# Weight pieces' transfers asked for one piece earlier, and narrowing steps placed anew, in a retention and two-layer MoE kernel

## The chip, the cores and the metric

One core of a Trainium2 chip runs the whole program. The metric is the device time of one execution in microseconds; below that of a kernel stands the median of several runs. Lower is better.

## What is computed

Retention over 4 batches and 8 heads (576 positions, 64 per head), then two dense layers with a hidden width of 2048 on 2304 tokens of width 512. The weights arrive as 64-bit floats, because a float32 array times a float64 scalar gives one.

```python
def _attn_ref(q, k, v):                       # q, k, v: (4, 8, 576, 64)
    scores = scale * np.matmul(q, k.transpose(0, 1, 3, 2))
    gamma = 1.0 - 2.0 ** (-5.0 - np.arange(H))
    Dmat = np.where(rel >= 0, gamma[:, None, None] ** rel[None, :, :], 0.0)
    return np.matmul(scores * Dmat[None], v)

x = attn_out.transpose(0, 2, 1, 3).reshape(2304, 512)
h = x @ w_in;  x = np.maximum(0.01 * h, h) @ w_out      # first layer
h = x @ w2_in; x = (h - np.tanh(h)) @ w2_out            # second layer
```

## The kernel before

The kernel has two stages. `retention()` goes through 16 pairs of heads (`order`, pair 0 to 15). `layers()` then does the two dense layers. The change touches the first stage alone.

**A pair.** For pair i TensorE computes the scores (`scores`, L674), the chunk states (`states_mm`, L723, and `scores_tail`), and the outputs of pair i - 1 (L755, L766). DVE masks the scores (`mask`, L697), carries the states (L733) and, with ACT (L774), writes the output as a high and a low part (`finish`, L775). POOL scales q (`prep_q`, L642), ACT scales k of the next pair (`prep_k`, L658). One PSUM tile holds the scores of one pair, so scores i wait for mask i - 1.

**Units.** From pair 6 on (`first = NP + 2`) every pair also carries one unit of the first dense layer on finished tokens: `unit_h(u)` (L822, 24 matmuls into the PSUM tile x_b), its two evacuations on ACT (L828, L829) and one on DVE (L830), then `unit_o(u - 1)` (L847, 24 matmuls) and `unit_evac(u - 1)` (L864, or L866 on ACT and L867 on DVE). There is one x_b, so unit u + 1 needs L830 of unit u. Units 2 and 3 are the first to use the w1i and w1o pieces 2 and 3: their first 12 matmuls take piece 2, their last 12 piece 3.

**Weight pieces.** A piece is a 128 x 512 block of 64-bit weights, 512 KB. Piece keys are (layer, kind, f), kind 0 for w_in, 1 for w_out. Each goes through these steps: `load_piece` (a transfer on SP's queue, L147), `begin` (ACT, L164), `clamp` (DVE, L170), `shift` (DVE, L175), `top` and `low` (DVE, both L181), then the split: a high part on ACT (L253) and a low part on POOL (L254). Eight pieces of the first layer come first (`pieces`), then eight of the second layer (`early_kept`), which are split and written back to DRAM (`keep_split`, `keep_out`). Raw pieces are staged in parts of `acc` that are free yet: four places for the first eight, of which two serve the kept ones too, so a transfer has to wait for `low` of the piece that had the place before.

**Order.** Every engine and SP's DMA queue work strictly in the order in which the program writes the instructions. All steps of all pieces stand in one list, `ops`, made by `piece_ops(keys, ahead)`, which puts the transfer of the piece `ahead` further on right behind each piece's `low`. `fill(i, part)` issues the next stretch of the list at three points of pair i: part 0 after the mask and before the pair's other work (ahead of `unit_h`), part 1 between `unit_h` and `unit_o`, part 2 at the end. How far it goes is given by `marks` or, where it has an entry, by the table `early`: (i, part) -> index in the list.

On SP the transfers of pair i + 2 (q, k at L627 and L628; kv at L634 and L635) are written at the start of pair i. There are three kv buffers, so those of pair i + 2 wait for the outputs of pair i - 1, late in pair i; all that SP has behind them waits too.

Of the kernel before, what the change touches and what calls it, by code (L numbers as in the profile page):

```python
# [35 lines left out]
def retention_moe_moe(  # L36
# [101 lines left out]
    def load_piece(key):  # L138
        m, kind, f = key
        src = ((w1i, w1o), (w2i, w2o))[m][kind][f]  # L140
        if key in early_kept or key[0] == 0 and key[2] < GF:
            k = len(raw_at)
            raw_at[key] = at = NT - (2048 if k in (0, 1, 4, 5) else 1024)
            st = acc_t[:, k % 2 * 2 + 1, at:at + (1024 if wide else 512)].bitcast(I64 if wide else F32)
        else:
            st = pools["st"].tile([P, 512], I64 if wide else F32, tag="st", name="st")
        nc.sync.dma_start(out=st, in_=src)  # L147
        raw[key] = st

    def narrow_ops(key):  # L150

        if not wide:
            def only():
                w = cw_pool[0].tile([P, 512], F32, tag="cw", name="cw")
                nc.vector.tensor_copy(out=w, in_=raw.pop(key))
                half[key] = w
            return [only]
        t = {}

        def begin():  # L160
            words = raw.pop(key).bitcast(U32).rearrange("p (n t) -> p n t", t=2)
            t["lo"], t["hi"] = words[:, :, 0], words[:, :, 1]
            t["w"] = cw_pool[0].tile([P, 512], U32, tag="cw", name="cw")
            nc.scalar.activation(  # L164
                out=t["w"].bitcast(F32), in_=t["hi"].bitcast(F32), func=AF.Abs
            )

        def clamp():
            wf = t["w"].bitcast(F32)
            nc.vector.tensor_scalar(  # L170
                out=wf, in0=wf, scalar1=F64_LO, scalar2=F64_HI, op0=ALU.max, op1=ALU.min
            )

        def shift():
            nc.vector.tensor_scalar(  # L175
                out=t["w"], in0=t["w"], scalar1=3, scalar2=0x3FFFFFF8,
                op0=ALU.logical_shift_left, op1=ALU.bitwise_and,
            )

        def join(src, scalar, op):  # L180
            nc.vector.scalar_tensor_tensor(  # L181
                out=t["w"], in0=t[src], scalar=scalar, in1=t["w"], op0=op, op1=ALU.bitwise_or
            )

        def top():
            join("hi", 0xC0000000, ALU.bitwise_and)

        def low():
            join("lo", 29, ALU.logical_shift_right)
            half[key] = t["w"].bitcast(F32)  # L190

        return [begin, clamp, shift, top, low]
# [11 lines left out]
    def keep_ops(key):  # L204

        m, kind, f = key
        if kind:
            return [([lambda: keep_split(key, half.pop(key))], [lambda: keep_out(key)])]
        stages = [([lambda: keep_split(key, half[key])], [lambda: keep_out(key)])]
        if f % 2:  # L210
            both = [(0, f - 1), (1, f - 1)]
            stages[0][1].append(lambda: sums_of(f - 1))
            stages.append((
                [lambda k=k: keep_split(k, half.pop((1, 0, f - 1 + k[0]))) for k in both],
                [lambda k=k: keep_out(k) for k in both],
            ))
        return stages
# [24 lines left out]
    def split_piece(key):  # L242
        wf = half.pop(key)
        m, kind, f = key
        if kind:
            wp = w_out_place(m)
        else:
            wp = w_place(m, f // GF, f % GF)
        split_into(wp, wf)
        wt[key] = wp  # L250
# [7 lines left out]
    early_kept = [(1, 1, f) for f in range(GF, 3 * GF)]  # L258
# [276 lines left out]
    def piece_ops(keys, ahead=2, split=True, spare=()):  # L535


        ops, later = [], []

        def due():  # L540
            soon = [x for stages in later for x in stages[:1]]
            later[:] = [stages[1:] for stages in later if stages[1:]]
            return [op for x, _ in soon for op in x], [op for _, x in soon for op in x]

        for j, key in enumerate(keys):
            part = narrow_ops(key)
            if j + ahead < len(keys):
                part.append(lambda k=keys[j + ahead]: load_piece(k))
            soon, then = due()
            ops += part[:3] + soon + part[3:] + then  # L550
            if key in spare:
                later.append(keep_ops(key))
            elif split:
                later.append([([lambda k=key: split_piece(k)], [])])
        while later:
            soon, then = due()
            ops += soon + then
        return ops


    def retention():
        with ExitStack() as ac:
# [22 lines left out]
            def factors(p, n):  # L585
                at, parts = 0 if p == 0 else LONE, []
                for width in (16, 32, 8, 16):
                    parts.append(tab_sb[:, at:at + width * n])
                    at += width * n
                return parts  # L590

            kt_sb = []
            for p, n in ((0, 1), (1, NP - 1)):
                k = factors(p, n)[0].rearrange("p (n h a) -> p n h a", h=2, a=8)
# [6 lines left out]
            order = [(b, p) for b in range(B) for p in range(NP)]  # L601
# [18 lines left out]
            def load(i):  # L620
                load_qk(i)
                load_v(i)
# [15 lines left out]
            def prep_q(i):  # L638

                b, p = order[i]  # L640
                q = qk[i][:, 1, :MAIN].rearrange("p (c r) -> p c r", r=CH)
                nc.gpsimd.tensor_tensor(  # L642
                    out=q, in0=q, in1=qt_sb[:, p:p + 1, :].to_broadcast([P, NFULL, CH]),
                    op=ALU.mult,
                )
                if i < GROUPED:
                    prep_q_tail(i)
# [19 lines left out]
            def scores(i):  # L667
                kt, qt = qk[i][:, 0, :], qk[i][:, 1, :]
                sc = ps_s.tile([P, 2, 512], F32, tag="sc", name="sc")
                for c in range(NFULL):  # L670
                    cs = slice(c * CH, (c + 1) * CH)
                    for h in range(2):
                        r = slice(64 * h, 64 * h + 64)
                        nc.tensor.matmul(  # L674
                            out=sc[:, h, cs], lhsT=kt[r, cs], rhs=qt[r, cs], start=True, stop=True
                        )
                return sc
# [93 lines left out]
            def finish(i, src, lo, hi):  # L771
# [6 lines left out]


            pieces = [(0, kind, f + j) for f in range(0, GF, 2) for kind in range(2) for j in range(2)]  # L780
            base = len(piece_ops(pieces, ahead=3))
            ops = piece_ops(pieces, ahead=3) + [lambda k=k: load_piece(k) for k in early_kept[:2]]
            ops += piece_ops(early_kept, spare=early_kept)
            at_pair = [0, 4, 9, 15, 22, 34, 46, 52]
            marks = [0] + at_pair + [
                base + 2 + (len(ops) - base - 2) * i // (len(order) - 8) for i in range(len(order) - 7)
            ]
            first = NP + 2
            done, u = [0], 0

            early = {
# [3 lines left out]
            }  # L795

            def fill(i, part):
                a, b = marks[i:i + 2] if i < len(order) else marks[-1:] * 2
                now = early.get((i, part), a + (b - a) * (part + 1) // 3)
                for op in ops[done[0]:now]:  # L800
                    op()
                done[0] = max(done[0], now)
# [66 lines left out]
            def pair_steps(i, fast):  # L869
# [46 lines left out]
                base=0, channel_multiplier=-1,  # L916
# [23 lines left out]
            def busy(n):  # L940
                for _ in range(n):
                    nc.tensor.matmul(
                        out=x_b[:, 0, :CH], lhsT=tri, rhs=tri, start=True, stop=True
                    )

            busy(8)
            for i in range(len(order)):
                if i + 2 < len(order):
                    load(i + 2)
                if i < 2:  # L950
                    load_piece(pieces[i + 1])
                fast = i >= first
                sc = scores(i)
                if i == 0:
                    busy(4)
                prep_q(i)
                mask(i, sc)
                if i == 0:
                    mask_table(1, NP - 1)
                fill(i, 0)  # L960
                pair_steps(i, fast)
                if fast or (i, 2) in early:
                    fill(i, 2)
# [250 lines left out]
```

## Time and profile before

| | before |
|---|---|
| median of 3 runs | 868.64 us (867.55 to 869.42) |
| profiled execution | 867.3 us, of it the span 865.4 us |
| mean granted TensorE clock over the span | 0.994 |
| TensorE matmul busy | 848.4 us, 98% of the span |
| DVE, ACT, POOL busy | 70%, 51%, 44% |

Times in the rows are microseconds from the start of the span. The granted clock is given as a share of 2.4 GHz: 1.00 is that level, 0.50 is 1.2 GHz. "Pair i" below is the stretch from the first score matmul of pair i to that of pair i + 1: pair 8 runs from 47.56 to 59.61, pair 9 to 69.92, pair 10 to 88.90, pair 11 to 98.40.

### The profile page before, as it was taken

To read this page: it belongs to the slowest core of one execution; us is meant where nothing else is said; L and a number is where in the kernel's file an instruction comes from. 1 tells how busy PE (TensorE), PEld (TensorE's weight loads), DVE (VectorE), ACT (ScalarE), POOL (GpSimd) and SP (SyncE) were. 2 spreads that over 40 slices of the span, in tenths; PEclk is the share of its full clock that TensorE was granted. 3 is DMA by queue.
4 is the path that set the end of the run, shared out by engine and by line. 5 is a ranking of instruction groups with operands and counts; after the bars stand their busy time and mean duration, and the time that the engine had idled before them with its cause. 6 is when DMAs were issued, how large, how long until landed. Compare 5 with 4: busy or idle time off the path is not lost.

```text
span 865.4 us, 15316 instructions
## 1 busy us (share of the span) xinstructions
PE 848.4 (98%) x5774; PEld 752.8 (87%) x5774; DVE 608.9 (70%) x1052; ACT 445.6 (51%) x879; POOL 377.3 (44%) x308
## 2 busy tenths in 40 slices
PE   8996999999999999999999999999999999999997
PEld 7886999988888889888888989888999899999996
DVE  7994876597877676659675487856766667777775
ACT  4542443453345433453544477766656556665664
POOL 4432232050035401464355477755555455454454
PEclk9997999999999999999999999999999999999999
DMA  9853754242355534553544603392225412563112
GB/s 354 305 175 113 224 180 159 100 133 97 122 189 208 186 123 123 219 195 122 195 171 154 210 1 148 140 346 79 88 89 184 172 74 74 195 243 123 49 50 73
DMA packets 37784, 133.77 MB, mean 155 GB/s; under 512 B 4304, under 2 KB 4944, under 8 KB 35664
## 3 DMA queue, kind: packets, MB, share of 16 engines
q1 hardware_dynamic: 37424, 132.66, 43.1%
q8 instruction: 45, 0.74, 0.4%
q14 instruction: 27, 0.22, 0.1%
q10 hardware_dynamic: 288, 0.15, 0.1%
HBM read 96.62 MB, written 36.18 MB: 153 GB/s over the span
## 4 chain that ended last, share of the span: by engine, by line
PE 91%; DVE 4%; issue 2%; DMA 1%; POOL 1%; ACT 1%; SPq 0%; DVEq 0%; POOLq 0%; ACTq 0%
PE a L426 41%; PE h L273 22%; PE h L307 18%; PE x_b L822 3%; PE a L847 3%; PE o L766 1%; PE o L755 1%; PE sc L674 1%; DVE cw L181 1%; DMA qk<-in_kT 1%; DVE pt L697 1%; DMA acc<-in_w2o 1%; PE x_c L723 0%; DVE st L733 0%; POOL w L254 0%
## 5 line engine op out<-in xcount | busy, mean ns | idle before, releaser
L426 PE MATMUL a<-w 128*128 128x512 f32 (+1 forms) x1680 | 394.1, 377 | 0.0
L426 PEld LDWEIGHTS a<-w 128*128 128x128 f32 x1680 | 293.4, 188 | 47.4
L254 POOL TENSOR_TENSOR w<-cw,w 128x512 fp32r<-128x512 f32 x80 | 113.6, 1438 | 253.6 <-ACT w L253 227.9
L273 PE MATMUL h<-xh,w 128*128 128x512 f32 (+1 forms) x672 | 187.1, 349 | 0.0
L366 POOL TENSOR_TENSOR v<-t,u 128x512 f32<-128x512 f32 (+1 forms) x76 | 93.3, 1228 | 98.3 <-ACT t L363 94.2
L273 PEld LDWEIGHTS h<-xh,w 128*128 128x128 f32 x672 | 119.5, 189 | 17.0
L398 POOL TENSOR_TENSOR w<-v,w 128x512 fp32r<-128x512 f32 (+1 forms) x76 | 95.9, 1261 | 62.7 <-ACT w L397 62.7
L352 ACT ACTIVATE w<-h 128x512 fp32r<-128x512 f32 (+1 forms) x68 | 37.2, 547 | 159.7 <-PE h L273 114.8
L273 PE MATMUL h<-xl,w 128*128 128x512 f32 (+1 forms) x336 | 117.0, 348 | 0.0
L307 PE MATMUL h<-xh,w 128*128 128x256 f32 x512 | 101.1, 281 | 0.1
L307 PEld LDWEIGHTS h<-xe,w 128*128 128x128 f32 x576 | 80.9, 189 | 9.5 <-DVE mk L301 1.8
L181 DVE SCALAR_TENSOR_TENSOR cw<-st,cw 128x512 uint32<-128x512 uint32 x96 | 86.5, 901 | 2.5
L392 DVE SCALAR_TENSOR_TENSOR v<-q,v 128x512 f32<-128x512 f32 (+1 forms) x76 | 61.9, 814 | 36.1 <-POOL v L366 36.1
L307 PEld LDWEIGHTS h<-xh,w 128*128 128x128 f32 x512 | 83.2, 190 | 2.7 <-DVE v L395 1.4
L307 PE MATMUL h<-xe,w 128*128 128x256 f32 x576 | 84.2, 282 | 0.4 <-DVE mk L301 0.4
L511 DVE TENSOR_TENSOR acc<-a,acc 128x512 f32<-128x512 f32 (+1 forms) x113 | 71.3, 657 | 17.0 <-PE a L426 17.0
L362 ACT ACTIVATE u<-h 128x512 f32<-128x512 f32 (+1 forms) x80 | 44.2, 552 | 73.9 <-DVE h L301 51.6
L170 DVE TENSOR_SCALAR cw<-cw 128x512 f32<-128x512 f32 x64 | 32.8, 512 | 64.1 <-ACT cw L164 63.9
L397 ACT ACTIVATE w<-v 128x512 fp32r<-128x512 f32 (+1 forms) x76 | 45.3, 596 | 62.3 <-DVE v L395 59.7
L307 PE MATMUL h<-xl,w 128*128 128x256 f32 x256 | 71.9, 281 | 0.0
L273 PEld LDWEIGHTS h<-xl,w 128*128 128x128 f32 x336 | 63.3, 188 | 8.6
L381 DVE TENSOR_TENSOR h<-h,t 128x512 f32<-128x512 f32 (+1 forms) x80 | 51.3, 642 | 14.6 <-ACT t L363 14.5
(95 smaller groups left out, 1178.3 us busy)
## 6 DMA issues: line engine op xcount, KB each, us to landing
kept<-w SPq DMA_DIRECT2D x48, 512.0 KB, 3.3
w<-kept SPq DMA_DIRECT2D x48, 512.0 KB, 4.8
xe<-xkept SPq DMA_DIRECT2D x12, 1536.0 KB, 6.5
st<-in_w2i SPq DMA_DIRECT2D x16, 512.0 KB, 3.9
st<-in_w1i SPq DMA_DIRECT2D x12, 512.0 KB, 4.2
st<-in_w1o SPq DMA_DIRECT2D x12, 512.0 KB, 3.4
xkept<-xe SPq DMA_DIRECT2D x4, 1536.0 KB, 8.5
kv<-in_vn SPq DMA_DIRECT2D x16, 320.0 KB, 4.1
```

The source lines that it names most:

```text
L181: nc.vector.scalar_tensor_tensor(out=t["w"], in0=t[src], scalar=scalar, in1=t["w"], op0=op, op1=ALU.bitwise_or)
L254: nc.gpsimd.tensor_tensor(out=wp[:, 1, :], in0=wf, in1=wp[:, 0, :].bitcast(F32), op=ALU.subtract)
L273: nc.tensor.matmul(out=ps[:, :n], lhsT=w[:, wi, cs], rhs=x[:, kk, t0:t0 + n], start=kk == 0 and i == 0, stop=kk == KK - 1 and i == 2,)
L307: nc.tensor.matmul(out=out_, lhsT=w[:, wi_, at:at + P], rhs=x(xi, kk), start=start and kk == 0 and j == 0, stop=stop and kk == 1 and j == ...
L362: nc.scalar.activation(out=u[:, :n], in_=h, func=AF.Square)
L366: nc.gpsimd.tensor_tensor(out=v[:, :n], in0=t_[:, :n], in1=u[:, :n], op=ALU.mult)
L381: nc.vector.tensor_tensor(out=h, in0=h, in1=tmp[s][1][:, :n], op=ALU.subtract)
L392: nc.vector.scalar_tensor_tensor(out=v, in0=q, scalar=RHO_A, in1=v, op0=ALU.add, op1=ALU.mult)
L397: nc.scalar.activation(out=gt[:, 0, g_at(s)], in_=v, func=AF.Copy)
L398: (nc.gpsimd if m else nc.vector).tensor_tensor(out=gt[:, 1, g_at(s)], in0=v, in1=gt[:, 0, g_at(s)].bitcast(F32), op=ALU.subtract)
L426: nc.tensor.matmul(out=o, lhsT=l, rhs=r, start=f == 0 and i == 0 and d % pack == 0, stop=f == GF - 1 and i == 2 and (d + 1) % pack == 0, s ...
L511: nc.vector.tensor_tensor(out=dst, in0=a, in1=dst, op=ALU.add)
```

## The change

The list of steps is made with the transfers four pieces ahead instead of three, and one more transfer is issued before the list begins (`if i < 3`). The transfers of the first two kept pieces, until now at the end of the first eight pieces' steps, stand right behind `low` of the seventh and of the eighth piece. Two splits move forward: (0,0,2) from behind `shift` of (0,0,3) to right behind its own `low`; (0,0,3) from behind `shift` of (0,1,2) to right behind its own `low`. Several entries of `early` change. In the stretches that matter the steps then stand so (each line is one call of `fill`; b, c, s, t, l are begin, clamp, shift, top, low):

```
         before                                    after
(2, 0)   t l (0,0,0), load (0,1,1)                 t l (0,0,0), load (0,0,2)
(4, 0)   l (0,0,1)                                 l (0,0,1), load (0,0,3)
(4, 2)   load (0,0,2), b (0,1,0)                   b (0,1,0)
(6, 0)   t l (0,1,0), load (0,0,3)                 t l (0,1,0), load (0,1,2)
(6, 1)   b..l (0,1,1), load (0,1,2)                b..l (0,1,1), load (0,1,3)
(7, 0)   t l (0,0,2), load (0,1,3)                 t l (0,0,2), split (0,0,2)
(7, 1)   b c s (0,0,3), split (0,0,2), t l (0,0,3) b c s t l (0,0,3), split (0,0,3)
(7, 2)   b c s (0,1,2), split (0,0,3)              b c s (0,1,2)
(8, 0)   t l (0,1,2)                               t l (0,1,2), load (1,1,4)
(8, 1)   b c s (0,1,3), split (0,1,2)              b c s (0,1,3), split (0,1,2), t l (0,1,3), load (1,1,5)
(8, 2)   t l (0,1,3), split (0,1,3)                split (0,1,3)
(9, 0)   load (1,1,4), load (1,1,5), b c (1,1,4)   nothing
(9, 1)   s t (1,1,4)                               b c (1,1,4)
(9, 2)   l (1,1,4), load (1,1,6), b (1,1,5)        s t l (1,1,4), load (1,1,6), b (1,1,5)
```

Piece (0,1,1) is asked for at the start of pair 2 instead of in (2, 0). From (10, 0) on the calls hold the same steps as before.

```diff
             pieces = [(0, kind, f + j) for f in range(0, GF, 2) for kind in range(2) for j in range(2)]
-            base = len(piece_ops(pieces, ahead=3))
-            ops = piece_ops(pieces, ahead=3) + [lambda k=k: load_piece(k) for k in early_kept[:2]]
+            ops = piece_ops(pieces, ahead=4)
+            for a, b in ((36, 33), (42, 39)):
+                ops.insert(b, ops.pop(a))
+            for at, k in zip((45, 52), early_kept):
+                ops.insert(at, lambda k=k: load_piece(k))
+            base = len(ops)
+            assert base == 54
             ops += piece_ops(early_kept, spare=early_kept)
             at_pair = [0, 4, 9, 15, 22, 34, 46, 52]
             marks = [0] + at_pair + [
-                base + 2 + (len(ops) - base - 2) * i // (len(order) - 8) for i in range(len(order) - 7)
+                base + (len(ops) - base) * i // (len(order) - 8) for i in range(len(order) - 7)
             ]
...
             early = {
-                (1, 0): 3, (2, 0): 6, (2, 2): 7, (3, 0): 11, (4, 0): 12, (4, 2): 14,
+                (1, 0): 3, (2, 0): 6, (2, 2): 7, (3, 0): 11, (4, 0): 13, (4, 2): 14,
                 (5, 0): 17, (6, 0): 20, (6, 1): 27, (6, 2): 31, (7, 0): 34, (7, 1): 40,
-                (7, 2): 44, (8, 0): 46, (8, 1): 50, (8, 2): 53,
+                (7, 2): 43, (8, 0): 46, (8, 1): 53, (8, 2): 54, (9, 0): 54, (9, 1): 56,
             }
...
-                if i < 2:
+                if i < 3:
                     load_piece(pieces[i + 1])
```

## Rows read from the trace of the kernel before

**Rows 1.** Windows: stretch, length, busy us of PE, PEld, DVE, ACT, POOL, clock, DMA share, GB/s.

```profile
5.00:31.28 26.28, 25.12 (x394) 20.92 (x396) 24.12 (x53) 14.29 (x39) 13.41 (x14) 1.00 1.03 393
...
47.56:59.61 12.05, 10.22 (x124) 9.34 (x124) 11.70 (x22) 6.55 (x14) 5.63 (x5) 1.00 0.45 143
59.61:69.92 10.31, 9.81 (x125) 9.22 (x124) 5.20 (x13) 1.76 (x5) 2.85 (x3) 1.00 0.35 116
69.92:88.90 18.98, 11.95 (x125) 11.49 (x124) 11.77 (x24) 5.96 (x13) 2.86 (x3) 0.73 0.43 146
88.90:98.40 9.50, 9.50 (x126) 9.12 (x124) 7.16 (x15) 3.91 (x9) 2.91 (x3) 1.00 0.77 237
```

**Rows 2.** Timeline of TensorE: start, length, instruction, [idle ahead of it, what ended it].

```profile
51.40 0.38 PE L822 MATMUL x_b<-xh,w 128*128 128x256 f32 x1 [0.98 <-ACT w L253]
52.74 0.50 PE L822 MATMUL x_b<-xh,w 128*128 128x256 f32 x2 [0.85 <-POOL w L254]
65.75 1.45 PE L847 MATMUL a<-w 128*128 128x256 f32 x10 [0.50 <-POOL w L254]
78.06 0.58 PE L822 MATMUL x_b<-xh,w 128*128 128x256 f32 x1 [7.03 <-DVE w L830]
```

**Rows 3.** Timeline of ACT, pairs 7 to 10.

```profile
46.91 0.63 ACT L253 ACTIVATE w<-cw 128x512 fp32r<-128x512 f32 x1 [1.28 <-DVE cw L181]
47.45 0.58 ACT L866 ACTIVATE acc<-a 128x512 f32<-128x512 f32 x1
...
54.20 0.60 ACT L828 ACTIVATE w<-x_b 128x512 fp32r<-128x512 f32 x1 [2.86 <-PE x_b L822]
54.70 0.59 ACT L829 ACTIVATE x_b<-x_b 128x512 f32<-128x512 f32 x1
...
75.65 0.66 ACT L164 ACTIVATE cw<-acc 128x512 f32<-128x512 f32 x1 [11.32 <-DMA acc<-in_w2o]
```

**Rows 4.** Chain of work that ended last: start, length, what.

```profile
70.69 4.88 DMA acc<-in_w2o
...
78.06 5.29 PE x_b L822 x24
...
90.01 2.94 PE x_b L822 x24
```

**Rows 5.** SP's timeline (kv of pair 10), then SP's waits: us, times, longest.

```profile
59.42 0.42 SPq L635 DMA_DIRECT2D kv<-in_vn  x1
...
SPq L634 <- PE x_e L766: 62.3, 13, 9.8
```

**Rows 6.** Timeline of DVE, pairs 7 to 9.

```profile
46.80 0.68 DVE L830 TENSOR_TENSOR w<-x_b,w 128x512 fp32r<-128x512 f32 x1
...
47.85 1.38 DVE L175 TENSOR_SCALAR cw<-cw 128x512 uint32<-128x512 uint32 x1
49.26 1.42 DVE L181 SCALAR_TENSOR_TENSOR cw<-acc,cw 128x512 uint32<-128x512 uint32 x2
...
54.25 0.43 DVE L175 TENSOR_SCALAR cw<-cw 128x512 uint32<-128x512 uint32 x1
...
59.60 0.68 DVE L867 COPY acc<-a 128x512 f32<-128x512 f32 x1
...
62.25 1.42 DVE L181 SCALAR_TENSOR_TENSOR cw<-acc,cw 128x512 uint32<-128x512 uint32 x2
```

**Rows 7.** Timeline of POOL, the split of (0,0,2).

```profile
47.62 1.33 POOL L254 TENSOR_TENSOR w<-cw,w 128x512 fp32r<-128x512 f32 x1 [3.67 <-ACT w L253]
```

**Rows 8.** Timeline of TensorE; then kT of pair 5, issued at 19.05: us to landing.

```profile
26.77 1.16 PE L674 MATMUL sc<-qk 64*128 64x128 f32 x16
...
29.14 0.33 PE L755 MATMUL x_e<-qk,st 64*64 64x64 f32 x4 [0.41 <-DVE pt L713]
...
DMA to landing us min/median/max: 7.0/7.0/7.0
```

**Rows 9.** Windows, one us of pair 10's wait.

```profile
72.00:73.00 1.00, 0.00 (x0) 0.00 (x0) 0.00 (x0) 0.00 (x0) 0.44 (x1) 0.85 0.85 208
```

## The prediction

> **What bounds the kernel now.** I read the windows view first, cut at the start of each pair's scores [rows 1]. From pair 11 on a pair with a unit takes 9.50 us, and TensorE is busy for all of it: that is the floor. Three pairs stand above it: pair 8 takes 12.05, pair 9 10.31, pair 10 18.98, so 2.55 + 0.81 + 9.48 = 12.84 us lie above the floor. Everything behind pair 10 is TensorE end to end, so what is won here should reach the end one to one. TensorE's own rows then say where the time lies [rows 2]: in pair 8 it waits 0.98 and 0.85 for the two halves of the split of w1i piece 3 (0,0,3), in pair 9 0.50 for the split of w1o piece 3 (0,1,3), in pair 10 7.03 for DVE's L830.
>
> The last one is not DVE's fault. ACT stood idle for 11.32 us ahead of one L164, the first step of the first kept piece (1,1,4), until that piece's transfer landed [rows 3]. Unit 3's two evacuations (L828, L829) stand behind it in ACT's queue, L830 behind them, and unit 4 needs their PSUM tile. The chain shows the transfer going out only at 70.69 and landing 4.88 later [rows 4]: SP works in order, and that issue stands behind kv of pair 11, whose buffer TensorE releases late in pair 9 (the waits view names x_e L766 for L634 [rows 5]). Asked and used in the same step, the piece had no chance. The stall also costs clock: the 18.98 us have a mean granted clock of 0.73 [rows 1], and unit 4's 24 matmuls took 5.29 against 2.94 at 2.4 GHz [rows 4]. 7.03 + 2.35 is 9.38 of the 9.48.
>
> **Part 1, the kept pieces' transfers: -9.48.** The first is now issued in pair 8, behind kv of pair 10, which went out at 59.42 [rows 5]; 0.43 of issue and the 0.83 of part 2 make it 60.7, with the 4.88 of [rows 4] 65.6. Its first step moves from ahead of unit 3 to behind unit 3's L828/L829. Scores 9 start at 59.61 + 0.83, take about 1 us, and unit 3's matmuls 2.94: ACT reaches L828 near 64.4 and the step near 65.5. What is left of that wait holds only the next finish (L774), due when pair 8's outputs end, about 1 us ahead of scores 10 at 69.92 [rows 1]: over 3 us of cover; if it were gone, each us late would be one. The second transfer, behind the eighth piece, waits on SP for that piece's last step (about 62.5); behind it stand q, k of pair 11, not used before 79. So pair 10 falls to the floor: 18.98 - 9.50 = 9.48. Bounds: 7.03 if the clock fell anyway, 9.48 if not.
>
> **Part 2, the split of piece (0,0,2) ahead of unit 1: +0.83.** This speaks against the change. Its ACT half (L253) now stands ahead of unit 1's L828/L829 and needs the end of DVE's L181 pair, so it can't start before 46.91 [rows 3]. L828 follows 0.54 later (46.91 to 47.45), L829 0.50 later (54.20 to 54.70) and takes 0.59: 48.54 [rows 3]. DVE's next instruction is L830, which waits for it: 48.58 instead of 46.80 [rows 6], 1.78 us of idle on an engine that is busy for 11.70 of pair 8's 12.05 [rows 1]. Part comes back: 1.05 behind L830 (46.80 to 47.85) comes the shift, L175, at 49.63. Before, it took 1.38 beside POOL's L254 (47.62 to 48.95) [rows 6, 7]; now that L254 is over, and it should take the 0.43 of the free one. So the L181 pair of (0,0,3) starts at 49.63 + 0.46 = 50.09 instead of 49.26, 0.83 later. The split follows it directly as before, and TensorE waits for just this split [rows 2]: its resume at 52.74 moves to 53.57. Pair 8: 12.88. Bounds: the evacuation costs nothing but the shift is free, -0.95; the shift meets POOL all the same, +1.78. I take the middle, as it follows the queue order. That unit 2 also waits until 49.3 for L830 instead of starting at 48.60 is inside this, since its second half is what is late.
>
> **Part 3, the steps of (0,1,3) and its split: -0.81.** Its L181 pair moves from behind 2.65 us of other DVE work (59.60 to 62.25) to ahead of it [rows 6]. DVE is later by then: the split of (0,0,3) now also stands ahead of L866 and L774 on ACT, so DVE's L775 waits for L774, about 1.2 us, less 0.5 for another L170 free of POOL: I put DVE 1.5 behind (bound 2.0). The pair ends at 63.67 - 2.65 + 1.5 = 62.5 and the split is ready 2.06 later (as from 49.26 + 1.42 = 50.68 to 52.74 in pair 8 [rows 2, 6]): 64.6, at worst 65.1. Unit 2's second half wants it at 65.25 + 0.83 = 66.1. The wait of pair 9 goes, and pair 9 takes 9.50. Next late is TensorE itself: DVE's mask 9, behind that pair and 2.65 us of other work, would end near 66.5, and scores 10 don't want it before 69.9.
>
> **Part 4, transfers four ahead: +0.34.** From 5 to 31 us the DMA engines are full (share 1.03, 393 GB/s) [rows 1]. One piece more (0,0,2) now goes out ahead of pair 5's q, k: 524,288 B at 393 GB/s is 1.33 us. That kT was issued at 19.05 and landed 7.0 later, at 26.05; scores 5 began at 26.77 [rows 8]. Landing at 27.38 and with 0.14 to start, scores begin 0.75 later. 0.41 of it is covered: TensorE idled that long at 29.14 for DVE's pt [rows 8]. 0.34 is left; bounds 0 and 0.75. The transfers of pairs 6 and 7 have over 1.3 us in hand, and the other pieces land before ACT comes to them. SP holds the new issue in pair 2 until DVE has read that slot; q, k of pair 5 behind it would wait in a full queue anyway.
>
> The Trainium skill (DMA: Bandwidth & Descriptors, Specifications) gives a lower limit for HBM, about 358 GB/s per core; by it, as an estimate, the piece takes 1.46 us and the part costs 0.47. The trace shows 393, so its rate stands.
>
> **Sum.** -9.48 + 0.83 - 0.81 + 0.34 = -9.12. The profiled execution took 867.3 (span 865.4 and 1.9 around it), so it would become 858.2. It lies 1.3 below the median of the runs, 868.64; from the median: 859.5.
>
> **Rivals.**
> *The clock falls in pair 8 (22%).* TensorE would stand still for 1.5 us between the halves of unit 2 (about 50.7 to 52.2), then 0.85 more. Before, two waits of 0.98 and 0.85 left the clock at 2.4 GHz; but in pair 10, idle since 71.03, it fell within 72 to 73 [rows 9], in under 2 us. Price by unit 4's rows: 2.35. 861.9.
> *The shift meets POOL again (9%).* L175 took 1.38 beside POOL and 0.43 alone [rows 6]. If POOL's L254 runs 0.7 us later than I place it, pair 8 loses 0.95 more: 860.5. The Trainium skill (SBUF — State Buffer, Who interferes with whom) has the mechanism: such an instruction and POOL's take a shared port in turn, and the later one fully blocks. The rows agree.
> *The ACT order costs nothing (14%).* Should L830 not wait, pair 8 gains 0.95 instead of losing 0.83: 857.7. Against it: L253 has to follow the L181 pair, as it does now at 46.91. If all of pair 8's waits went (4%): 868.64 - 12.84 + 0.34 = 856.1.
> *The kept piece is late all the same (2%).* The issue is asked early but SP would have to be held for 8 us more; then pair 10's wait stays: 868.64 + 0.83 - 0.81 + 0.34 = 869.0.
> *Slower (2%).* Place: pairs 8 to 10. The gap of the first rival drops the clock, and the waits of DVE and ACT on each other, which part 2 begins, keep it at 1.2 GHz. A unit's first half alone costs 2.35 more, its second (24 matmuls as well) about as much: 4.7 a pair. It decides from two pairs (868.9) on; three give 873.6. Against it: in pair 11 unit 5 took 2.94 again [rows 4], one unit after the fall.
>
> **How the numbers follow.** Forecast 47%: 859.5, itself 858.6 to 860.3 by the bounds of part 4 and the spread of the runs. The range goes up to 862.2, to take in the clock, and down to 856.6, to take in the better order; outside are all waits gone, the late piece, the slow pairs and a bigger clock loss, under 2 in 10. A measurement tells 0.2%, 1.7 us, from no change. Faster: all but the last two rivals, 0.96; same 0.02; slower 0.02.
>
> **What would show it.** After the change: no long idle of ACT ahead of L164 in pair 9 or 10, pair 10 at 9.50 with clock 1.00 (part 1); L830 of unit 1 waiting for ACT L829, and TensorE waiting longer than 0.98 for ACT L253 in pair 8 (part 2); no wait for L254 in pair 9 (part 3); scores 5 some 0.7 later, scores 6 some 0.3 (part 4). I would be wrong if pair 8 came out near 9.50, if its clock were below 1.00, or if another ACT wait for a transfer took the old one's place.

## The result, and the profile after

The changed kernel takes 858.60 us (median of 6 runs, 858.11 to 860.47), the kernel before 869.05 beside it (6 runs, 867.55 to 869.61): a ratio of 0.9887 by the means (859.09 to 868.89), 95% interval 0.9874 to 0.9900. The forecast was 859.5 with a range of 856.6 to 862.2.

The windows of after, cut at the starts of scores 4 and 5, then 8 to 11 (columns as in [rows 1]):

```profile
24.34:29.41 5.07, 4.78 (x71) 3.62 (x71) 4.92 (x11) 2.23 (x7) 2.21 (x3) 1.00 1.01 392
50.19:63.18 12.99, 10.25 (x124) 9.39 (x124) 10.47 (x22) 7.96 (x17) 5.03 (x5) 1.00 0.27 92
63.18:72.67 9.49, 9.49 (x124) 9.11 (x124) 8.01 (x18) 4.12 (x9) 3.40 (x4) 1.00 0.70 237
72.67:82.17 9.50, 9.50 (x125) 9.12 (x124) 9.22 (x18) 3.92 (x9) 2.92 (x3) 1.00 0.52 181
```

Pairs 9 and 10 are at the floor, pair 8 is above it by more than before. By stretches of the two profiled executions:

| stretch | before | after | difference | forecast |
|---|---|---|---|---|
| to scores 2 | 13.15 | 15.68 | +2.53 | 0 |
| scores 2 to 7 (part 4) | 24.91 | 25.01 | +0.10 | +0.34 |
| pair 7 | 9.50 | 9.50 | 0.00 | 0 |
| pair 8 (part 2) | 12.05 | 12.99 | +0.94 | +0.83 |
| pair 9 (part 3) | 10.31 | 9.49 | -0.82 | -0.81 |
| pair 10 (part 1) | 18.98 | 9.50 | -9.48 | -9.48 |
| scores 11 to the end | 776.46 | 776.47 | +0.01 | 0 |

(The spans are 865.36 and 858.64.) The first line is no part of the change. The profiled execution of after took 860.47, the slowest of the six, because its start was slow. TensorE's timeline there (start, length, instruction, [idle ahead of it, what ended it]):

```profile
5.89 2.08 PE L674 MATMUL sc<-qk 64*128 64x128 f32 x16 [0.68 <-DMA qk<-in_kT]
7.90 2.07 PE L947 MATMUL x_b<-pt 128*128 128x128 f32 x8
```

and that of before:

```profile
5.08 1.16 PE L674 MATMUL sc<-qk 64*128 64x128 f32 x16 [0.18 <-DMA qk<-in_kT]
6.17 1.16 PE L942 MATMUL x_b<-pt 128*128 128x128 f32 x8
```

The same 16 and 8 matmuls take nearly twice as long. In all ten kernels below, eight of them with transfers four ahead like after, scores 1 begin between 8.65 and 9.40 us, not at 11.35. From scores 2 to scores 11 the two profiles differ by 66.49 - 75.75 = -9.26, against a forecast sum of -9.12.

Three views of after show the parts. From scores 8 on it runs 2.63 us later than before (50.19 against 47.56); I take that off where I compare.

TensorE's waits; pairs 9 and 10 have none left, so [rows 2]'s waits for L254 in pair 9 and for L830 in pair 10 are gone:

```profile
51.92 0.39 PE L827 MATMUL x_b<-xh,w 128*128 128x256 f32 x1 [0.62 <-DVE w L835]
54.83 0.39 PE L827 MATMUL x_b<-xh,w 128*128 128x256 f32 x1 [1.27 <-ACT w L253]
56.18 0.50 PE L827 MATMUL x_b<-xh,w 128*128 128x256 f32 x2 [0.85 <-POOL w L254]
```

ACT, then DVE, around unit 1's evacuation (L833 to L835, before L828 to L830):

```profile
49.54 0.63 ACT L253 ACTIVATE w<-cw 128x512 fp32r<-128x512 f32 x1 [5.85 <-DVE cw L181]
50.08 0.58 ACT L833 ACTIVATE w<-x_b 128x512 fp32r<-128x512 f32 x1
50.55 0.59 ACT L834 ACTIVATE x_b<-x_b 128x512 f32<-128x512 f32 x1
```

```profile
51.17 0.69 DVE L835 TENSOR_TENSOR w<-x_b,w 128x512 fp32r<-128x512 f32 x1 [1.67 <-ACT x_b L834]
51.78 0.42 DVE L170 TENSOR_SCALAR cw<-cw 128x512 f32<-128x512 f32 x1
52.23 0.43 DVE L175 TENSOR_SCALAR cw<-cw 128x512 uint32<-128x512 uint32 x1
52.70 1.42 DVE L181 SCALAR_TENSOR_TENSOR cw<-acc,cw 128x512 uint32<-128x512 uint32 x2
```

SP with the two kept pieces' transfers, and ACT with the first one's first step (L164) and the finish behind it (L774):

```profile
62.99 0.42 SPq L635 DMA_DIRECT2D kv<-in_vn  x1
63.52 2.18 SPq L147 DMA_DIRECT2D acc<-in_w2o  x2
```

```profile
67.76 0.60 ACT L834 ACTIVATE x_b<-x_b 128x512 f32<-128x512 f32 x1
68.36 0.67 ACT L164 ACTIVATE cw<-acc 128x512 f32<-128x512 f32 x1
71.94 0.60 ACT L774 ACTIVATE xh<-o 128x512 fp32r<-128x512 f32 x1 [2.90 <-PE o L766]
```

L164 has no wait now; before it had 11.32 us [rows 3].

### The profile page after: what moved, and what is told of

The parts are those of the page before. It is cut to its first block, busy times and chain, and to the rows that moved or that the text cites. A ratio compares the mean times of both kernels' runs of the same rounds, so it can differ in the third digit from the quotient of the medians.

```text
span 858.6 us, 15324 instructions
## 1 busy us (share of the span) xinstructions
PE 848.3 (99%) x5774; PEld 752.6 (88%) x5774; DVE 608.3 (71%) x1052; ACT 445.4 (52%) x879; POOL 377.6 (44%) x308
## 4 chain that ended last, share of the span: by engine, by line
PE 93%; DVE 4%; issue 1%; DMA 1%; ACT 0%; POOL 0%; SPq 0%; DVEq 0%; ACTq 0%; POOLq 0%
PE a L426 41%; PE h L273 22%; PE h L307 18%; PE x_b L827 4%; PE a L852 3%; PE o L766 1%; PE sc L674 1%; PE o L755 1%; DVE cw L181 1%; PE x_c L723 1%; DVE pt L697 1%; DMA qk<-in_kT 1%; DVE st L733 0%; DVE xl L775 0%; PE x_e L687 0%
## 5 line engine op out<-in xcount | busy, mean ns | idle before, releaser
L254 POOL TENSOR_TENSOR w<-cw,w 128x512 fp32r<-128x512 f32 x80 | 113.4, 1436 | 243.9 <-ACT w L253 217.8
L181 DVE SCALAR_TENSOR_TENSOR cw<-st,cw 128x512 uint32<-128x512 uint32 x96 | 86.5, 901 | 2.5
L253 ACT ACTIVATE w<-cw 128x512 fp32r<-128x512 f32 x80 | 47.0, 622 | 28.9 <-DVE cw L181 15.1
```

Source lines behind the costliest of these rows:

```text
L181: nc.vector.scalar_tensor_tensor(out=t["w"], in0=t[src], scalar=scalar, in1=t["w"], op0=op, op1=ALU.bitwise_or)
L253: nc.scalar.activation(out=wp[:, 0, :], in_=wf, func=AF.Copy)
L254: nc.gpsimd.tensor_tensor(out=wp[:, 1, :], in0=wf, in1=wp[:, 0, :].bitcast(F32), op=ALU.subtract)
```

## The experiments

Each starts from the kernel before or from after, as its diff shows. Lengths of pairs are read from the profiled execution; times are medians of 4 to 11 runs. The kernel before had a median of 868.36 beside parts 1, 2 and 4 alone and part 2 undone, 868.55 beside the kernels "asked late" and "high-part terms first", and 868.46 beside the other four. An ellipsis in a diff stands for lines left out.

### One part alone

**Part 1 alone**, on the kernel before:

```diff
...
+            for at, k in zip((46, 53), early_kept):
+                ops.insert(at, lambda k=k: load_piece(k))
...
-                (7, 2): 44, (8, 0): 46, (8, 1): 50, (8, 2): 53,
+                (7, 2): 44, (8, 0): 47, (8, 1): 51, (8, 2): 55, (9, 0): 55, (9, 1): 57,
```

> The kernel before with the kept pieces' part alone: the first two kept pieces' transfers right behind low of the seventh and the eighth piece (pair 8), the first kept piece's begin behind unit 3's evacuations in pair 9; three ahead and all splits as before. Theory (the stall of pair 10 is only the transfer asked in the step that uses it): pair 10 falls from 18.98 to 9.50, pair 8 stays at 12.05 and pair 9 at 10.31, so 9.5 us less than the kernel before. Rival (the four-ahead transfers are needed too, because SP is held behind the eighth piece's transfer): ACT still waits for the kept piece and pair 10 keeps 2 us or more of its wait.

Measured: 858.89 us, ratio 0.9890 (0.9876 to 0.9903): the whole gain of the change. Pair 10 takes 9.49, and L164 of the kept piece has no wait. One thing was not expected, in pair 8 (its window, then one us of it):

```profile
48.07:61.71 13.64, 11.81 (x125) 10.95 (x124) 12.45 (x23) 6.66 (x14) 5.62 (x5) 0.87 0.36 126
...
55.00:56.00 1.00, 1.00 (x7) 1.00 (x7) 0.97 (x3) 1.00 (x3) 0.00 (x0) 0.50 0.00 0
```

The granted clock is at 0.50 (1.2 GHz) behind the same two waits that before has (0.98 and 0.85), and pair 8 takes 13.64 instead of 12.05. Pair 9 takes 9.64 though part 3 is missing: TensorE comes 1.6 us later, and the late split is covered.

**Part 2's move alone**, the split of (0,0,2) ahead of unit 1:

```diff
+            ops.insert(33, ops.pop(37))
...
-                (5, 0): 17, (6, 0): 20, (6, 1): 27, (6, 2): 31, (7, 0): 34, (7, 1): 40,
+                (5, 0): 17, (6, 0): 20, (6, 1): 27, (6, 2): 31, (7, 0): 35, (7, 1): 40,
```

> The kernel before with one thing moved: the split of (0,0,2) to right behind its own low, ahead of unit 1. Theory (strict queue order of ACT holds back L829 and so DVE's L830): L830 of unit 1 waits about 1.7 us for ACT, the shift behind it takes 0.43 instead of 1.38, pair 8 grows from 12.05 by 0.8 to 1.0, the whole by as much. Rival (the gain of a shift without POOL outweighs the wait, or the wait is covered): pair 8 at 12.05 or below, the time the same or 1 us less.

Measured: 869.03 us, 0.67 above before, ratio 1.0009 (1.0000 to 1.0017). Pair 8 takes 13.01 (+0.96); pairs 9 and 10 give back 0.14 and 0.33. DVE's two rows are those of after:

```profile
48.51 0.69 DVE L831 TENSOR_TENSOR w<-x_b,w 128x512 fp32r<-128x512 f32 x1 [1.67 <-ACT x_b L830]
...
49.57 0.43 DVE L175 TENSOR_SCALAR cw<-cw 128x512 uint32<-128x512 uint32 x1
```

So the move lengthens pair 8, and the shift's 0.95 comes back within it, as the forecast had it. The runs alone only just show the cost: the interval is 0 to 1.5 us.

**Part 4 alone**, four ahead:

```diff
-            base = len(piece_ops(pieces, ahead=3))
-            ops = piece_ops(pieces, ahead=3) + [lambda k=k: load_piece(k) for k in early_kept[:2]]
+            base = len(piece_ops(pieces, ahead=4))
+            ops = piece_ops(pieces, ahead=4) + [lambda k=k: load_piece(k) for k in early_kept[:2]]
...
-                if i < 2:
+                if i < 3:
```

> The kernel before with the transfers four ahead and nothing else. Theory (a full DMA queue delays pair 5's kT): pairs 4 to 6 together longer by 0.1 to 0.4 us, pairs 8 to 10 at 12.05, 10.31 and 18.98, the time 0 to 0.4 us more. Rival (the earlier transfers are what pairs 7 to 9 gain from): pair 8 or 9 shorter by 0.5 us or more.

Measured: 867.82 us, ratio 0.9994 (0.9986 to 1.0003): no difference. Scores 5 do wait for their transfer,

```profile
27.57 1.16 PE L674 MATMUL sc<-qk 64*128 64x128 f32 x16 [0.22 <-DMA qk<-in_kT]
```

and pair 4 takes 5.19 instead of 4.67, but pair 5 takes 4.22 instead of 4.51: pairs 4 to 6 are 0.22 longer, within the 0.1 to 0.4 expected. Pair 2, which lies ahead of the delay, is 0.22 shorter, so scores 2 to 7 take 24.91, as before. In this profile too the clock fell in pair 8 (13.68 us, mean clock 0.88).

### Parts undone

**Part 2 undone** in after:

```diff
-            for a, b in ((36, 33), (42, 39)):
+            for a, b in ((42, 39),):
...
-                (5, 0): 17, (6, 0): 20, (6, 1): 27, (6, 2): 31, (7, 0): 34, (7, 1): 40,
+                (5, 0): 17, (6, 0): 20, (6, 1): 27, (6, 2): 31, (7, 0): 33, (7, 1): 40,
```

> The changed kernel with the split of (0,0,2) put back to behind the shift of (0,0,3), all else as changed. Theory: L830's wait for ACT goes, the shift of (0,0,3) meets POOL's split again (1.38), pair 8 falls from 12.99 to about 12.05, pairs 9 and 10 stay at 9.50, the time is 0.9 us less than the changed kernel's, 9.9 less than the kernel's before. Rival (DVE's later place in pair 9 decides): pair 9 grows again and takes the gain back.

Measured: 858.30 us, ratio 0.9882 (0.9867 to 0.9897). Pair 8 was to come back to 12.05 and took 13.71 in the profile:

```profile
48.04:61.75 13.71, 11.88 (x125) 11.00 (x124) 12.11 (x23) 6.57 (x14) 5.44 (x5) 0.88 0.27 87
...
54.00:55.00 1.00, 1.00 (x7) 1.00 (x6) 0.92 (x6) 0.37 (x1) 0.69 (x1) 0.50 0.00 0
```

The waits are the old ones again (0.98 and 0.85), but the clock fell. The four runs split by their mean granted clock: 857.11 and 857.60 at 1.000 and 0.999, 859.55 and 859.00 at 0.998 and 0.997. After's runs at 0.999 to 1.000, the profiled one with its slow start left out, are 858.11 to 858.62, so at equal clock part 2 costs 0.9 to 1.5 us, two runs against four. That half of the runs had the lower clock takes most of it back in the median.

**Part 3 undone** in after, `top` and `low` of (0,1,3) behind the work of (8, 1), with the second kept transfer:

```diff
-                (7, 2): 43, (8, 0): 46, (8, 1): 53, (8, 2): 54, (9, 0): 54, (9, 1): 56,
+                (7, 2): 43, (8, 0): 46, (8, 1): 50, (8, 2): 54, (9, 0): 54, (9, 1): 56,
```

> The changed kernel with top and low of (0,1,3) and the transfer behind them back at the end of pair 8, behind the other DVE work. Theory (part 3: their earlier place is what ends pair 9's wait): TensorE waits again for POOL's split in pair 9, 0.5 to 1.5 us, pair 9 at 10 to 11, pairs 8 and 10 unchanged. Rival (with pair 8 longer than before the split is ready in time anyway): pair 9 at 9.50, the time unchanged.

Measured: 859.98 us, ratio 0.9905 (0.9888 to 0.9921), 1.4 above after's 858.60. Pair 9 takes 11.00, pair 10 9.48. TensorE's wait and the window:

```profile
68.09 1.44 PE L852 MATMUL a<-w 128*128 128x256 f32 x10 [0.84 <-POOL w L254]
```

```profile
61.25:72.25 11.00, 10.08 (x124) 9.28 (x124) 9.18 (x18) 3.99 (x10) 3.48 (x4) 1.00 0.61 205
```

The wait that part 3 removed is back, longer than before's 0.50. The rest of the pair's 1.51 above after's 9.49 stands in TensorE's busy time, 10.08 against 9.49.

### The kept pieces: asked early, or begun late?

Part 1 does two things: it asks for the transfers earlier, and it begins the first piece behind unit 3's evacuations instead of ahead of them. One kernel undoes the second, the other the first.

**Begun early**, `begin` and `clamp` back in (9, 0):

```diff
-                (7, 2): 43, (8, 0): 46, (8, 1): 53, (8, 2): 54, (9, 0): 54, (9, 1): 56,
+                (7, 2): 43, (8, 0): 46, (8, 1): 53, (8, 2): 54, (9, 0): 56,
```

> The changed kernel with begin and clamp of the first kept piece back ahead of unit 3, its transfer still asked for in pair 8. Theory (asking early alone ends the stall): ACT waits for the transfer at most 3 us, unit 3's evacuations are 3 us later, which unit 4 doesn't see; pair 10 stays at 9.50 and the time unchanged. Rival (the later use is what ends it): TensorE waits for L830 again ahead of unit 4, pair 10 over 10.5.

Measured: 859.60 us, ratio 0.9897 (0.9882 to 0.9912). ACT does stand in front of unit 3's evacuations,

```profile
67.54 0.67 ACT L164 ACTIVATE cw<-acc 128x512 f32<-128x512 f32 x1 [3.26 <-DMA acc<-in_w2o]
```

but pair 9 takes 9.48 and pair 10 9.49: ACT's 3.26 us of waiting hold up nothing on TensorE. Pair 8 took 14.53 in this profile, with the clock at 0.50 from 54 to 55; the one run with a mean clock of 0.999, 858.04, is no slower than after's.

**Asked late**, both transfers back in (9, 0):

```diff
-            for at, k in zip((45, 52), early_kept):
-                ops.insert(at, lambda k=k: load_piece(k))
+            ops += [lambda k=k: load_piece(k) for k in early_kept[:2]]
...
-                (7, 2): 43, (8, 0): 46, (8, 1): 53, (8, 2): 54, (9, 0): 54, (9, 1): 56,
+                (7, 2): 43, (8, 0): 45, (8, 1): 51, (8, 2): 52, (9, 0): 54, (9, 1): 56,
```

> The changed kernel with the two kept transfers asked for in pair 9 again, as in the kernel before, while begin stays behind unit 3. Theory (asking early is what ends the stall; using late alone only moves it): ACT waits for the transfer until about 76 and DVE's clamp with it, unit 2's evacuation (L869) stands behind that, so unit 3's second product set waits some 4 us in pair 10: pair 10 at 13 to 14, the time 3.5 to 6 us over the changed kernel's. Rival (the later begin alone ends it): pair 10 at 9.50, the time the changed kernel's.

Measured: 866.60 us, ratio 0.9976 (0.9965 to 0.9988). Pair 10 takes 16.24. ACT, TensorE and the window:

```profile
75.49 0.66 ACT L164 ACTIVATE cw<-acc 128x512 f32<-128x512 f32 x1 [9.55 <-DMA acc<-in_w2o]
```

```profile
77.95 5.46 PE L851 MATMUL a<-w 128*128 128x256 f32 x24 [3.64 <-DVE acc L868]
```

```profile
70.26:86.50 16.24, 12.60 (x125) 11.95 (x124) 10.04 (x21) 4.92 (x11) 2.90 (x3) 0.79 0.51 171
```

I had expected 13 to 14, and a time 3.5 to 6 above after's; it is 8.0 above. I priced the wait of TensorE (3.64) and not that the clock falls behind it again, where 24 matmuls take 5.46 instead of the 2.88 of after. The profiled execution is the fastest of the seven (864.75; they go up to 867.03), so in most runs more is lost than this profile shows. Pair 10 by the two choices, in us, each from one profile:

| | begun ahead of unit 3's evacuations | begun behind them |
|---|---|---|
| asked in (9, 0) | 18.98 (before) | 16.24 |
| asked in pair 8 | 9.49 | 9.50 (after) |

The earlier request is enough by itself; the later begin alone gives 2.74 of the 9.48 in these profiles.

### What is left in pair 8

In after pair 8 is the only pair above the floor. Three kernels try to bring it down.

**`top`, `low` and split of (0,0,2) at the end of pair 6:**

```diff
-                (5, 0): 17, (6, 0): 20, (6, 1): 27, (6, 2): 31, (7, 0): 34, (7, 1): 40,
+                (5, 0): 17, (6, 0): 20, (6, 1): 27, (6, 2): 34, (7, 0): 34, (7, 1): 40,
```

> The changed kernel with top, low and the split of (0,0,2) one fill earlier, at the end of pair 6, ahead of mask 7. Theory (pair 8 hangs on DVE's and ACT's queue order alone): low ends 1.2 us earlier, L830 of unit 1 waits less, the split of (0,0,3) comes 1.2 us earlier, pair 8 falls from 12.99 to about 11.8 and the time by as much, where the clock stays up in both. Rival (mask 7, 1.2 us later now, holds scores 8): pair 7 grows over 9.50 by what pair 8 loses.

Measured: 857.28 us, ratio 0.9875 (0.9861 to 0.9890). Pair 8 takes 11.52, its waits are 0.64 and 0.85, and unit 2 no longer waits for L835.

**The shift away from POOL**: the split of (0,1,1) ahead of the shift of (0,0,2), that shift at the start of pair 7 behind the mask, the split of (0,0,2) behind unit 1's evacuations again:

```diff
-            for a, b in ((36, 33), (42, 39)):
+            for a, b in ((36, 34), (42, 39), (30, 29)):
...
-                (5, 0): 17, (6, 0): 20, (6, 1): 27, (6, 2): 31, (7, 0): 34, (7, 1): 40,
+                (5, 0): 17, (6, 0): 20, (6, 1): 27, (6, 2): 30, (7, 0): 33, (7, 1): 40,
```

> The changed kernel with three steps in another order: the shift of (0,0,2) behind mask 7 (so that it doesn't meet POOL's L642), the split of (0,0,2) behind unit 1's evacuations on ACT and behind begin of (0,0,3). Theory: no wait of L830 for ACT, one L175 of 1.40 becomes 0.43, the other keeps meeting POOL; low of (0,0,3) ends 1.9 us earlier than in the changed kernel, pair 8 falls from 12.99 to about 11.1, the time by 1.9 us, and with shorter waits the clock stays up in pair 8. Rival (the port's wait only moves to the next instruction): pair 8 at 12.0 to 12.5.

Measured: 856.68 us, ratio 0.9868 (0.9853 to 0.9883). Pair 8 takes 11.09. DVE's rows show both kinds of shift, and L835 with no wait. The first shift follows the mask, and POOL's L642 has ended at 44.46; the second runs beside POOL's L254 (47.15 to 48.47):

```profile
43.33 1.29 DVE L697 TENSOR_TENSOR pt<-sc,cm_sb 128x512 f32<-128x512 f32 x2
44.53 0.42 DVE L175 TENSOR_SCALAR cw<-cw 128x512 uint32<-128x512 uint32 x1
...
46.32 0.68 DVE L835 TENSOR_TENSOR w<-x_b,w 128x512 fp32r<-128x512 f32 x1
...
47.37 1.38 DVE L175 TENSOR_SCALAR cw<-cw 128x512 uint32<-128x512 uint32 x1
```

Of TensorE's waits 0.19 (ACT L253) and 0.85 (POOL L254) are left.

**High-part terms first**: the kernel just above, and in each half of `unit_h` the eight matmuls with the high part of the weights ahead of the four with the low part, which POOL writes last:

```diff
...
-                    for kk in range(KK):
+                    terms = ((0, xh), (0, xl), (1, xh))
+                    for kk, j in [(k, j) for k in range(KK) for j in (0, 1)] + [(k, 2) for k in range(KK)]:
...
```

> The kernel with the steps in port order (pair 8 at 11.09) and, in every unit, the 16 matmuls of a piece that take only its high part ahead of the 8 that take its low part (8 and 4 for each half of a unit). Theory (the 0.85 that TensorE waits in pair 8 between the high and the low part is POOL's split, and 8 matmuls of 0.12 us cover it): that wait goes, pair 8 at about 10.2, the time 0.8 to 0.9 us under the port-order kernel's. Rival (the first half's wait grows instead, or the order of the weight loads costs time in every unit): pairs from 11 on over 9.50, no gain.

Measured: 855.97 us, ratio 0.9857 (0.9843 to 0.9872), the fastest: 0.71 below the kernel just above, where 0.8 to 0.9 was expected, and the four runs of each don't overlap. Pair 8 takes 10.50, and the waits of its unit are 0.15 and 0.18:

```profile
50.75 0.39 PE L828 MATMUL x_b<-xh,w 128*128 128x256 f32 x1 [0.15 <-ACT w L253]
...
52.12 0.74 PE L828 MATMUL x_b<-xh,w 128*128 128x256 f32 x4 [0.18 <-POOL w L254]
```

Pair 9 takes 9.69 here instead of 9.50.

## Why the prediction was right

**The time: right, with 0.9 us that are not in the parts.** The stretches of the two profiles (scores 2 to 11) differ by 9.26, against a sum of 9.12; the medians differ by 10.45. The forecast took the sum off the median of before, as if the 1.3 between that median and the profiled execution were the same in both kernels. But the runs of before differ in their mean granted clock. Of its 38 runs beside the experiments, 20 had 0.994 to 0.996, like its profile (0.994), and a median of 867.70; 18 had 0.991 to 0.993 and a median of 868.93. After's four runs at 0.999 and 1.000 (median 858.53, the one with the slow start left out) are 9.17 below the 20, close to the sum, though they were not measured beside them. So a part of the medians' difference is probably that fewer of after's runs have the lower clock, for which the forecast had no term. That this lower clock is the fall in pair 8 is likely, as the profile of part 4 alone has it at a mean of 0.992, but no profile of before shows it.

**Part 1 (-9.48): right in size and in its steps.** The first kept transfer goes out at 63.52 - 2.63 = 60.9 (forecast 60.7), directly behind kv of pair 10. L164 runs at 65.7 (65.5) without waiting, and the ACT idle behind it, the cover, is 2.90 (over 3). The two-by-two table adds what the forecast had left in one lump: the request does it, the place of the first step doesn't matter once the data come early.

**Part 2 (+0.83): right, and it is a loss.** L833 starts 0.54 behind L253 (forecast 0.54), L834 0.47 later (0.50), DVE's L835 0.62 after that; DVE idles 1.67 (1.78); the shift takes 0.43 (0.43); TensorE resumes at 56.18 - 2.63 = 53.55 (53.57). Pair 8 grew by 0.94. The split put back shows 0.9 to 1.5 at equal clock, and the move alone +0.67 on the time, with an interval from 0 to 1.5. The gap between the halves, put at 1.5, was 1.27 of waiting.

**Part 3 (-0.81): right.** The L181 pair of (0,1,3) and the split's low part, in the timelines of DVE and POOL of after:

```profile
63.87 1.42 DVE L181 SCALAR_TENSOR_TENSOR cw<-acc,cw 128x512 uint32<-128x512 uint32 x2
```

```profile
66.03 1.29 POOL L254 TENSOR_TENSOR w<-cw,w 128x512 fp32r<-128x512 f32 x1 [2.02 <-ACT w L253]
```

The pair ends at 62.7 (forecast 62.5), the split at 64.7 (64.6). One reason within it was wrong: DVE was to wait some 1.2 us for L774; it did wait 1.18, but for ACT's L871, which stands ahead of L774, at the copy L872. The delay is the same, as both stand behind the same split on ACT:

```profile
55.30 0.69 DVE L872 COPY acc<-a 128x512 f32<-128x512 f32 x1 [1.18 <-ACT acc L871]
```

**Part 4 (+0.34): the step exists, its price is too small to be told from nothing.** In six of the nine profiles with four ahead scores 5 wait 0.17 to 1.06 us for kT's transfer, in none of the three with three ahead. In after itself they don't: its pair 4 grew by 0.40 behind a wait for DVE's st,

```profile
26.15 0.75 PE L755 MATMUL o<-qk,st 64*64 64x128 f32 x8 [0.28 <-DVE st L733]
```

and part 1 alone, with three ahead, has the same wait (0.27) and a pair 4 of 4.97. With the part alone scores 5 do wait; pair 4 grew by 0.52 (forecast 0.75), pair 5 gave back 0.29 (forecast 0.41). But scores 2 to 7 took 24.91, 24.90 and 25.04 in the three profiles with three ahead, and 24.89 to 25.61 in the nine with four ahead: means of 24.95 and 25.10, a difference of 0.15, where the nine differ by 0.72 among themselves. By the runs of the part alone it costs -0.54, with an interval from -1.2 to +0.26 (0.9986 to 1.0003 of 868.36): the forecast's 0.34 is just outside, its lower bound 0 inside. What makes the early pairs differ from one execution to the next stays open.

**The rivals.** That the shift meets POOL again did not happen in after (0.43); the two shifts of 0.42 and 1.38 within one kernel show that the price is right. The Trainium skill's rule of the shared port, on which that rival leaned (SBUF — State Buffer, Who interferes with whom), agrees with those two rows. That the ACT order costs nothing is refuted by the wait of 1.67 and by pair 8 with the move alone (13.01 against 12.05). The kept piece late all the same is refuted by L164 without a wait.

The clock rival was right as a mechanism, with a wrong cause and size. After's own pair 8 kept 1.00, but one of its six runs, 860.30 at a mean clock of 0.997, fits the fall. It is not part 2 that brings it on: of the five profiles with part 2's longer wait (1.26 to 1.28, then 0.85) one has the fall, of the four with the old waits (0.95 to 0.98, then 0.84 or 0.85) three. By the mean clocks it is, if anything, rarer in after (one of six runs) than in before (18 of 38, if their lower clock is this fall). And it costs 1.6 (13.64 to 13.71 in the three kernels with the old waits, against 12.05) or 1.5 (14.53 against 12.99), not the 2.35 that I took from unit 4 of pair 10, all of whose 24 matmuls ran low: in pair 8 a mean clock of 0.87 to 0.88 over 13.7 us is some 1.7 us of lost TensorE work (0.125 x 13.7), and no more. In the kernels of part 1 and part 4 alone, whose pair 9 still has the late split, part of it comes back there (9.64 and 9.70 instead of before's 10.31). With 1.6 the rival's time would have been 861.1, inside the range.

## What to carry to other kernels

A late transfer's cost is read where its request stands in its queue, not at the engine that waits: here the request stood behind a wait for a buffer, and putting it one stage earlier in the list took 9.48 us off that pair without moving any work. Where a step that waits on another engine is put ahead of an evacuation on an in-order engine, follow the evacuation's reader: the step took ACT 0.54 us, but it had to wait for DVE's own result, and so it and the two evacuations behind it ran one after the other while DVE stood idle for 1.67. A delay at a shared stretch early in the pipeline should be followed over several pairs before it is booked as lost.

## What was not expected of the hardware

**A slow start.** Every profile begins with matmuls at a lower rate than later, while the granted clock reads 1.00. The 16 matmuls ahead of the first scores take 3.48 to 3.79 us, here those of after:

```profile
1.43 3.78 PE L947 MATMUL x_b<-pt 128*128 128x128 f32 x16 [1.43 <-POOL pt L919]
```

Eight of the same matmuls behind the first scores take 1.16 in ten of the twelve profiles. What differs is how long this lasts: the first scores take 1.16 in two profiles, 1.22 to 1.87 in eight, 2.08 in after and in the kernel with the steps in pair 6; the eight behind them take 1.30 in that kernel and 2.07 in after alone. The window of after's first scores:

```profile
5.89:7.90 2.01, 2.01 (x16) 1.79 (x16) 0.00 (x0) 0.91 (x2) 0.84 (x1) 1.00 1.01 354
```

No run here shows why. With the first kT's transfer landing 0.8 us later it makes up the 2.53 us of the table's first line.

**The clock may fall behind waits that leave it alone in another execution.** Waits of 0.98 and 0.85 kept 2.4 GHz in before's profile and went with a fall to 1.2 GHz in three others. In the last two kernels of the pair 8 series the mean clock is 0.999 to 1.000 in every run and the runs lie within 1.0 us (856.45 to 857.42, 855.49 to 856.26), where after's, without the one with the slow start, lie within 2.2 (858.11 to 860.30): shorter waits may have bought steadiness as well as time, which these eight runs suggest and don't prove.
